# Router logits by token quarter: sixteen accumulating products of 64 columns in place of four of 256 and a summing product

## The chip, the cores and the metric

The kernel runs on one core of one Trainium2 chip. The metric is the time of one execution on the device, in microseconds (us); lower is better. A core has a matrix engine (TensorE: PE for its matmuls and PEld for its weight loads in the profile), a vector engine (DVE), a scalar engine (ACT), GpSimd (POOL), a queue that issues transfers (SyncE, SP), and 16 DMA engines. TensorE reads on-chip memory (SBUF) and writes only accumulators (PSUM, in banks of 512 float32 columns by 128 partitions).

## What is computed

Two stages: a decaying linear attention over 4 batches, 8 heads, 768 positions and head size 64, and a top-1 mixture of 8 experts over its 3072 output rows of 512 features.

```python
for t in range(S):                                   # attention, per batch and head
    state = gamma * state + outer(k[t], v[t])
    y[t] = scale * q[t] @ state
x = y.transpose(0, 2, 1, 3).reshape(3072, 512)

logits = normalized(x) @ normalized(expert_emb).T / tau
expert = argmax(logits, axis=1)                      # one expert for each row
gate = softmax(logits)[expert]
out[rows of e] = gate * (relu(x[rows of e] @ w1[e]) @ w2[e])
```

## The kernel before, in words

The attention stage works in 12 steps `m` (three for each batch, `NCB` = 3) of 256 tokens each. In a step TensorE transposes `k` and `q` of the next step (L365, L383), makes masked scores (L396, masked on DVE at L417), multiplies them with `v` (`intra`, L464), adds what the state contributes (`inter`, L471, recorded at L464 too) and adds to the states (`state`, L431). The result of step `m` is `yTs[m]`, 512 features (4 chunks `j` of 128, on the partitions) by 256 tokens. From there it goes two ways: DVE turns it into rows (`rows_turn`, L493), which SP writes to the buffer `xd` in DRAM (`rows`, L500); and the router works on it.

The router has three parts. `logits_products(m)` (L513) multiplies `enT`, the normalised expert embeddings (128 features by 32 columns of which 8 are experts) with `yTs[m]`. Chunk `j` of the features uses column quarter `j` of the array (32 of 128 columns), so its product of 32 by 256 lands in partitions 32j to 32j+31 of one bank; the four products are partial sums and each is a matmul on its own. `logits_rows(m)` (L521) turns the bank in blocks of 32 by 32 on DVE, so that the tokens come to the partitions: `parts`. `sums(g)` (L531) adds the four partial sums for a group `g` of steps (`GROUPS`: steps 0-2, 3-5, 6-7, 8, 9-10, 11): its left operand `quarters` is a constant of zeros and ones that adds the four partition blocks, and each of its four matmuls writes one quarter of the tokens. `choose` (L545 to L554) then finds maximum and argmax on DVE, `add_counts` (L572 to L576) counts, `count` and `ranks` (L561 to L565 on TensorE, L583 to L588 on DVE, one step later) give each row a slot in its expert's list, and `place` (L597, POOL) writes the row's number to the table `tbl` in DRAM.

All five engines run an order written out by hand; nothing is rearranged. In step `m` TensorE's order is: `count` of the group before, scores, `inter`, `state(m+1)`, `logits_products(m-1)`, transposes of `k`, `q`, `q`, `k` for `m+1`, `sums` if a group ended with step `m-1` (steps 3, 6, 8, 9, 11), then `intra(m)`. In step 3 the products of steps 0, 1 and 2 come together. In step 11 there are no transposes, and `sums` stands between the two halves of `intra`. DVE's order in a step is: `ranks`, masks, `logits_rows`, the sums of states (L444 to L449), `choose`, `add_counts`, `rows_turn(m-1)`.

SP's order matters at the end of the stage. In step 8 it issues the four writes of `rows(7)`, then 12 weight transfers of expert 0 (`load_piece`, L206), then a load of the first slot list (`early_slots`, L635), the writes of `rows(8)`, and two further slot lists. POOL then gathers the first 280 rows of expert 0 from `xd` (`early_gather`, L626, three gathers into `xge`), and SP's next weight transfers (L206, at 109.12 us) are held back until these gathers have landed. TensorE goes on with the transposes of `xge` (L645), the last `logits_products`, and the first layer of expert 0 (L260); from there the seven other experts follow.

Some PSUM room beside the states, `spare(u, j)`, is used as scratch for the router (the names `pst` of `sums`, `choose`, `count`).

Of the kernel before, what the change touches and what calls it, by code (L numbers as in the profile page):

```python
# [11 lines left out]
F32 = mybir.dt.float32  # L12
# [5 lines left out]
ALU = mybir.AluOpType  # L18
AX = mybir.AxisListType
# [5 lines left out]
P = 128  # L25
B, H, S, D = 4, 8, 768, 64
T2 = 2 * P
NCB = S // T2
NM = B * NCB
NB = 2 * NM  # L30
NT = B * S
DM = H * D
NE = 8
DF = 1024
KT = DM // P
FT = DF // P
Q = 32
NQ = P // Q
# [18 lines left out]
NOV = (NT - OV + P - 1) // P  # L57
# [3 lines left out]
def _layout():  # L61
    at, n = {}, 0
    for name, w in (("tq", NCB * 2 * H), ("tk", NCB * 2 * H), ("e16", NE), ("tok", 3),
                    ("ids", 2 * NB), ("quarters", Q), ("ovthr", NOV), ("caps", NE), ("order", NE), ("ranks", NE - 1)):
        at[name] = (n, n + w)
        n += w
    return at, n
# [7 lines left out]
def _constants():  # L75
    c = np.zeros((P, _CW), np.float64)
    p = np.arange(P)
    u, pl = p // 64, p % 64
    g = 1.0 - 2.0 ** (-5.0 - np.arange(H))

    def put(name, a):
        lo, hi = _AT[name]
        c[:, lo:hi] = np.broadcast_to(a, (P, hi - lo))

    t = (T2 * np.arange(NCB)[None, :, None, None] + (P * u + 2 * pl)[:, None, None, None]
         + np.arange(2)[None, None, :, None]).astype(np.float64)

    tt = (T2 * np.arange(NCB)[None, :, None, None] + (8 * (p // KT))[:, None, None, None]
          + np.arange(8)[None, None, None, :]).astype(np.float64)
    gg = g[(2 * (p % KT))[:, None] + np.arange(2)[None, :]][:, None, :, None]  # L90
    put("tq", (gg ** tt / np.sqrt(D)).reshape(P, -1))
    put("tk", (g ** -t).reshape(P, -1))
    put("e16", (np.arange(NE) / 16.0)[None, :])
    put("tok", p[:, None] + P * np.arange(3)[None, :])
    n = np.arange(NB)[None, :]
    put("ids", np.stack([(8 * (p % Q) + p // Q)[:, None] + T2 * (n // 2) + NQ * (n % 2),
                         (4 * (p % Q) + p // Q)[:, None] + P * n], 2).reshape(P, -1))
    put("quarters", (p % Q)[:, None] == np.arange(Q)[None, :])
    put("ovthr", (OV + P * np.arange(NOV))[None, :])
    put("caps", np.array(CAPS)[None, :])  # L100
    put("order", np.arange(NE)[None, :])
    put("ranks", np.array(RANKS)[None, :])
    tri = (p[:, None] < p[None, :]).astype(np.float16)
    return c.astype(np.float32), np.ascontiguousarray(tri)
# [3 lines left out]
def retention_moe(ctx: ExitStack, tc: tile.TileContext, q, k, v, emb, tau, w1, w2, const, const16, out):  # L108
    nc = tc.nc
# [9 lines left out]
    def C(name):  # L119
        lo, hi = _AT[name]  # L120
        return cst1[:, lo:hi] if hi <= _C1 else cst2[:, lo - _C1:hi - _C1]
# [386 lines left out]
    parts = {}  # L508

    def logits_products(m, ps=None):  # L510
        ps = pt_() if ps is None else ps
        for j in range(KT):
            nc.tensor.matmul(ps[j * Q:(j + 1) * Q, :T2], enT[:, j, :], yTs[m][:, j, :], start=True, stop=True,  # L513
                             skip_group_check=True)
        return ps

    def logits_rows(m, ps):
        g = group_of[m]
        if g not in parts:
            parts[g] = ap_.tile([P, max(map(len, GROUPS)), 2, NQ, Q], F32, name="parts")  # L520
        nc.vector.transpose(out=parts[g][:, m - GROUPS[g][0]].rearrange("p u g e -> p (u g) e"),  # L521
                            in_=ps[:, :T2].rearrange("p (g b) -> p g b", b=Q))

    def span(g):
        return slice(2 * GROUPS[g][0], 2 * GROUPS[g][-1] + 2)
# [1 line left out]
    def sums(g, ps=None, fresh=False, room=None):  # L527
        nm = len(GROUPS[g])
        ps = pt_() if ps is None else ps
        for i in range(NQ):  # L530
            nc.tensor.matmul(ps[i * Q:(i + 1) * Q, :2 * nm * NE], C("quarters"),  # L531
                             parts[g][:, :nm, :, i, :NE].rearrange("p m u e -> p (m u) e"), start=not fresh, stop=True,
                             skip_group_check=True)
        at = room if fresh else ps[:, 64:]
        return [a[:, :2 * nm * NE].rearrange("p (n e) -> p n e", e=NE) for a in (ps, at)] + [at[:, 48:48 + NE]]

    chosen = []

    def choose(g, zs):
        z, w, _ = zs  # L540
        r = span(g)
        nb = r.stop - r.start
        bc = lambda t: t.unsqueeze(2).broadcast_to([P, nb, NE])
        m = ap_.tile([P, nb], F32, name="m", bufs=1)
        nc.vector.tensor_reduce(out=m, in_=z, axis=AX.X, op=ALU.max)  # L545
        yield
        nc.vector.tensor_tensor(out=z, in0=z, in1=bc(m), op=ALU.subtract)
        yield
        nc.vector.scalar_tensor_tensor(out=w, in0=z, scalar=0.0,
                                       in1=C("e16").unsqueeze(1).broadcast_to([P, nb, NE]), op0=ALU.is_lt, op1=ALU.add)  # L550
        yield
        nc.vector.tensor_reduce(out=wmn[:, r], in_=w, axis=AX.X, op=ALU.min)
        yield
        chosen.append(nc.vector.tensor_tensor(out=oh[:, r], in0=w, in1=bc(wmn[:, r]), op=ALU.is_equal))  # L554
        yield
# [870 lines left out]
```

## Time and profile before

| | us |
|---|---|
| time, median of 3 runs | 398.85 (398.09 to 399.03) |
| the profiled execution, its own time | 397.74 |
| its span from the first to the last instruction | 395.9 |
| TensorE matmuls busy in the span | 385.1 (97%) |
| VectorE busy | 253.4 (64%) |
| ScalarE busy | 214.6 (54%) |
| GpSimd busy | 153.7 (39%) |

Times in the views count from the start of the span. A timeline row is: start, how long the merged instructions last from the first start to the last end, engine, line, operation, tiles (output <- inputs), shape, count, and in brackets the engine's idle time before it with what ended it. TensorE's matmuls overlap, so the distance from one row's start to the next row's start says what a row costs, not its length. One float32 matmul of the program shows as two records. The line number is that of the helper that records the instruction.

### The profile page before, as it was taken

The page shows a single profiled execution, that of the slowest core. Times are in us where ns is not written, and L with a number is a line of the kernel's source. Part 1 is how long each engine was busy: PE and PEld are TensorE (multiplying, and loading weights), DVE is VectorE, ACT ScalarE, POOL GpSimd, SP SyncE. Part 2 cuts the span into 40 slices and gives each one's busy share as a digit, 9 for nine tenths or more (in the row PEclk, how much of TensorE's full clock was granted, in tenths as well). Part 3 has the DMA queues.
Part 4 walks back from the last instruction along what each step waited for, and adds up shares of the span by engine and source line. Part 5 has one row for each costly group of instructions (what it writes and reads, how often), then busy time and mean ns, then how long its engine had stood idle before and what let it go on. Part 6 is the DMA issues. An engine that isn't in the chain of part 4 may idle for free.

```text
span 395.9 us, 9644 instructions
## 1 busy us (share of the span) xinstructions
PE 385.1 (97%) x3690; PEld 358.9 (91%) x3690; DVE 253.4 (64%) x534; ACT 214.6 (54%) x382; POOL 153.7 (39%) x176
## 2 busy tenths in 40 slices
PE   8999999999999899999999999999999999999993
PEld 4898888988889799999999999999899999999982
DVE  5596876979989358834861963766457656386300
ACT  4585576666847185518544744734855625464420
POOL 2956387688651515204702611520471221211230
PEclk9999999999999999999999999999999999999999
DMA  7998898797468867866868796796998747854121
GB/s 237 271 337 256 238 302 237 217 275 200 121 195 237 282 221 262 280 176 220 265 209 256 251 306 184 236 336 189 273 267 311 206 174 242 234 211 123 39 76 58
DMA packets 91012, 89.20 MB, mean 225 GB/s; under 512 B 10781, under 2 KB 69533, under 8 KB 90956
## 3 DMA queue, kind: packets, MB, share of 16 engines
q1 hardware_dynamic: 85916, 75.39, 63.7%
q0 software_dynamic: 4864, 13.03, 9.1%
q8 instruction: 31, 0.51, 0.5%
q14 instruction: 25, 0.20, 0.2%
q10 hardware_dynamic: 176, 0.07, 0.1%
HBM read 65.00 MB, written 18.79 MB: 212 GB/s over the span
## 4 chain that ended last, share of the span: by engine, by line
PE 82%; issue 7%; DVE 3%; DMA 3%; ACT 1%; POOL 1%; SPq 1%; POOLq 1%
PE b L260 11%; PE pst L1111 11%; PE py L260 9%; PE py L1111 9%; PE py L464 8%; PE pst L260 7%; PE b L396 6%; PE b L1111 4%; PE pst L1153 3%; PE pst L431 3%; PE b L365 3%; PE b L383 2%; DMA raw<-in_moe_w_dram 2%; PE pst L1193 2%; PE b L513 2%
## 5 line engine op out<-in xcount | busy, mean ns | idle before, releaser
L238 DVE TENSOR_TENSOR wlo<-raw,whi 128x1024 fp32r<-128x1024 f32 x64 | 77.7, 1218 | 16.9 <-ACT whi L234 16.5
L1135 POOL DMA_INDIRECT out_dram<-og,si x28 | 29.9, 1068 | 122.5 <-ACT og L1128 71.9
L234 ACT CAST whi<-raw 128x1024 fp32r<-128x1024 f32 x64 | 66.2, 1045 | 4.0 <-DMA raw<-in_moe_w_dram 4.0
L626 POOL DMA_INDIRECT xr<-xd,gi x25 | 30.6, 1223 | 31.7 <-ACT sq L293 15.3
L260 PE MATMUL b<-xh,whi 128*128 128x360 f32 (+5 forms) x104 | 34.3, 334 | 0.0
L260 PE MATMUL b<-xl,whi 128*128 128x360 f32 (+5 forms) x104 | 34.2, 333 | 0.0
L260 PE MATMUL b<-xh,wlo 128*128 128x360 f32 (+5 forms) x104 | 34.1, 332 | 0.0
L417 DVE TENSOR_TENSOR pm<-b,mask 128x512 f32<-128x512 f32 x48 | 29.8, 683 | 4.7 <-PE b L396 4.5
L1094 DVE STREAM_TRANSPOSE xt<-xg 128x384 f32<-128x384 f32 (+1 forms) x28 | 15.6, 578 | 25.5 <-DMA xg<-xs 25.5
L354 POOL TENSOR_TENSOR hh<-whi,cst 128x512 f32<-128x512 f32 x22 | 23.1, 1066 | 20.9 <-DVE pm L417 12.8
L265 ACT ACTIVATE hh<-b 128x360 fp32r<-128x360 f32 (+5 forms) x26 | 12.6, 484 | 33.1 <-PE b L260 33.1
L1111 PE MATMUL pst<-hh,whi 128*128 128x360 f32 (+4 forms) x88 | 29.4, 334 | 0.6 <-ACT hh L265 0.6
L1111 PE MATMUL pst<-hh,wlo 128*128 128x360 f32 (+4 forms) x88 | 29.4, 334 | 0.2 <-DVE wlo L238 0.2
L597 POOL DMA_INDIRECT tbl<-zt,sloti x24 | 25.4, 1056 | 10.8 <-issue 4.2
L1111 PE MATMUL pst<-hl,whi 128*128 128x360 f32 (+4 forms) x88 | 29.4, 334 | 0.1
L260 PE MATMUL py<-xl,whi 128*128 128x384 f32 (+5 forms) x84 | 27.9, 335 | 0.0
L260 PE MATMUL py<-xh,whi 128*128 128x384 f32 (+5 forms) x84 | 27.5, 334 | 0.0
L260 PE MATMUL py<-xh,wlo 128*128 128x384 f32 (+5 forms) x84 | 27.3, 331 | 0.0
L359 POOL TENSOR_TENSOR hl<-wlo,cst 128x512 f32<-128x512 f32 x22 | 22.7, 1047 | 7.8 <-DMA wlo<-in_k_dram 6.8
L396 PE MATMUL b<-qT,kT 64*128 64x128 f32 x384 | 24.7, 278 | 0.0
L464 PE MATMUL py<-pm,vs 128*64 128x128 f32 x384 | 24.1, 276 | 0.0
L1111 PE MATMUL py<-hh,whi 128*128 128x360 f32 (+4 forms) x72 | 23.5, 326 | 0.0
(236 smaller groups left out, 1010.4 us busy)
## 6 DMA issues: line engine op xcount, KB each, us to landing
raw<-in_moe_w_dram SPq DMA_DIRECT2D x60, 512.0 KB
whi<-in_q_dram SPq DMA_DIRECT2D x24, 256.0 KB
xd<-x SPq DMA_DIRECT2D x48, 128.0 KB
wlo<-in_k_dram SPq DMA_DIRECT2D x11, 512.0 KB
xs<-xr SPq DMA_DIRECT2D x6, 768.0 KB
og<-yt SPq DMA_DIRECT2D x72, 48.0 KB
whi<-in_v_dram SPq DMA_DIRECT2D x6, 512.0 KB
wlo<-in_v_dram SPq DMA_DIRECT2D x6, 512.0 KB
```

Of the source, the lines that this page charges most:

```text
L234: nc.scalar.copy(out=views[1], in_=views[0])
L238: nc.vector.tensor_tensor(out=views[2], in0=views[0], in1=views[1].bitcast(F32), op=ALU.subtract)
L260: nc.tensor.matmul(acc[:, :w], a, x[:, kt, cols], start=(n == 0), stop=(n == len(todo) - 1))
L354: return eng.tensor_tensor(out=qs_r[:, m % 3, :, a], in0=qin[m % 3][:, a], in1=w, op=ALU.mult)
L359: return eng.tensor_tensor(out=ks_r[:, m % 3, s, h], in0=kin[m % 3][:, h, s], in1=w[:, h], op=ALU.mult)
L396: nc.tensor.matmul(psc[a][:, j], kTs[m][a * D:(a + 1) * D, j, u].rearrange("p s c -> p (s c)"), q_cols(m, a, j, u), start=True, stop=True, ...
L417: o.append(nc.vector.tensor_tensor(out=pm, in0=psc[a], in1=w, op=ALU.mult))
L464: nc.tensor.matmul(pys[m][u][o * D:(o + 1) * D, j], lhsT, rhs, start=first, stop=True, skip_group_check=True)
L597: i = nc.gpsimd.indirect_dma_start(out=tbl[:, :], out_offset=bass.IndirectOffsetOnAxis(ap=sloti[:, n:n + 1], axis=0), in_=zt[:, n], in_off ...
L626: return nc.gpsimd.indirect_dma_start(out=xr[:n, j, :], out_offset=None, in_=xd[:rows_, :], in_offset=bass.IndirectOffsetOnAxis(ap=gi[:n, ...
L1111: nc.tensor.matmul(acc[:, :c], a[:, f], x[:, kt, :c], start=(n == 0), stop=(n == 3 * FT - 1))
L1135: i = nc.gpsimd.indirect_dma_start(out=out[:, :], out_offset=bass.IndirectOffsetOnAxis(ap=si[:n, e, j:j + 1], axis=0), in_=og[:n, j, :], i ...
```

## The change

`logits_products` now also splits the tokens: each of the four feature chunks `j` makes four matmuls, one for each quarter `i` of the tokens (64 columns: two blocks of 32, one of each half of the step), and quarter `i` of the array's columns always takes quarter `i` of the tokens. The four chunks add up in the accumulator (`start` at the first, `stop` at the last). So 16 matmuls of 64 columns stand where 4 of 256 stood, the bank holds 64 finished columns in place of 256 columns of partial sums, `logits_rows` turns 64 columns in place of 256, and `parts` is a quarter as large. `sums` makes no matmuls any more (4 in each of 6 groups are left out) and only hands out the scratch room. `choose` reads `parts` in SBUF where it read the sums in PSUM, and its row maxima `m` lie in PSUM scratch in place of SBUF. The constant `quarters` is left out.

```diff
     def logits_products(m, ps=None):
         ps = pt_() if ps is None else ps
         for j in range(KT):
-            nc.tensor.matmul(ps[j * Q:(j + 1) * Q, :T2], enT[:, j, :], yTs[m][:, j, :], start=True, stop=True,
-                             skip_group_check=True)
+            y = yTs[m][:, j].rearrange("p (u g b) -> p g u b", u=2, b=Q)
+            for i in range(NQ):
+                nc.tensor.matmul(ps[i * Q:(i + 1) * Q, :2 * Q].rearrange("p (u b) -> p u b", b=Q), enT[:, j, :], y[:, i],
+                                 start=(j == 0), stop=(j == KT - 1), skip_group_check=True)
         return ps
...
-            parts[g] = ap_.tile([P, max(map(len, GROUPS)), 2, NQ, Q], F32, name="parts")
-        nc.vector.transpose(out=parts[g][:, m - GROUPS[g][0]].rearrange("p u g e -> p (u g) e"),
-                            in_=ps[:, :T2].rearrange("p (g b) -> p g b", b=Q))
+            parts[g] = ap_.tile([P, max(map(len, GROUPS)), 2, Q], F32, name="parts")
+        nc.vector.transpose(out=parts[g][:, m - GROUPS[g][0]], in_=ps[:, :2 * Q].rearrange("p (u b) -> p u b", b=Q))
...
     def sums(g, ps=None, fresh=False, room=None):
         nm = len(GROUPS[g])
         ps = pt_() if ps is None else ps
-        for i in range(NQ):
-            nc.tensor.matmul(ps[i * Q:(i + 1) * Q, :2 * nm * NE], C("quarters"),
-                             parts[g][:, :nm, :, i, :NE].rearrange("p m u e -> p (m u) e"), start=not fresh, stop=True,
-                             skip_group_check=True)
         at = room if fresh else ps[:, 64:]
-        return [a[:, :2 * nm * NE].rearrange("p (n e) -> p n e", e=NE) for a in (ps, at)] + [at[:, 48:48 + NE]]
+        return [a[:, :2 * nm * NE].rearrange("p (n e) -> p n e", e=NE) for a in (ps, at)] + [at[:, 48:48 + NE], at[:, 56:56 + 2 * nm]]
...
     def choose(g, zs):
-        z, w, _ = zs
+        z, w, _, m = zs
...
-        m = ap_.tile([P, nb], F32, name="m", bufs=1)
-        nc.vector.tensor_reduce(out=m, in_=z, axis=AX.X, op=ALU.max)
-        yield
-        nc.vector.tensor_tensor(out=z, in0=z, in1=bc(m), op=ALU.subtract)
+        s = parts[g][:, :nb // 2, :, :NE].rearrange("p m u e -> p (m u) e")
+        nc.vector.tensor_reduce(out=m, in_=s, axis=AX.X, op=ALU.max)
+        yield
+        nc.vector.tensor_tensor(out=z, in0=s, in1=bc(m), op=ALU.subtract)
```

Nothing else moves: ACT, POOL and SP have the same instructions in the same order. Two places show it. The first is TensorE in step 8, from the products of step 7 to `intra` (`b` are banks, `hl` and `hh` the scaled `k` and `q`, `pst` the scratch). Before:

```order
L513 MATMUL b_1617<-yT,enT 32x256 x4
L365 MATMUL b_1627<-ident,hl 128x128 x4
L383 MATMUL b_1635<-ident,hh 128x128 x4
L383 MATMUL b_1641<-ident,hh 128x128 x4
L365 MATMUL b_1648<-ident,hl 128x128 x4
L531 MATMUL pst_1567<-parts,cst_61 32x32 x4
L464 MATMUL py_1519<-pm_1531,vs 64x128
```

and in the changed kernel (its line numbers are one to four off):

```order
L514 MATMUL b_1691<-yT,enT 32x64 x16
L364 MATMUL b_1713<-ident,hl 128x128 x4
L382 MATMUL b_1721<-ident,hh 128x128 x4
L382 MATMUL b_1727<-ident,hh 128x128 x4
L364 MATMUL b_1734<-ident,hl 128x128 x4
L463 MATMUL py_1593<-pm_1605,vs 64x128
```

The four summing matmuls between the last transposes and `intra` are gone, and the product has 16 short matmuls. The second place is DVE in the same step, from `logits_rows(7)` into `choose`. Before:

```order
L521 STREAM_TRANSPOSE parts<-b_1617 128x256
L446 COPY s_1623<-pst_1567 128x256
L449 TENSOR_TENSOR s_1625<-pst_1567,tB 128x256
L545 TENSOR_REDUCE m<-pst_1567 128x4
L547 TENSOR_TENSOR pst_1567<-pst_1567,m 128x32
L549 SCALAR_TENSOR_TENSOR pst_1567<-pst_1567,cst_61 128x32
```

and in the changed kernel:

```order
L522 STREAM_TRANSPOSE parts<-b_1691 128x64
L445 COPY s_1709<-pst_1641 128x256
L448 TENSOR_TENSOR s_1711<-pst_1641,tB 128x256
L541 TENSOR_REDUCE pst_1641<-parts 128x4
L543 TENSOR_TENSOR pst_1641<-parts,pst_1641 128x32
L545 SCALAR_TENSOR_TENSOR pst_1641<-pst_1641,cst_61 128x32
```

The order is the same, but the first instruction of `choose` reads what DVE itself wrote two instructions earlier, where it read what TensorE wrote.

## Rows read from the trace of the kernel before

**Rows 1.** Engines by stretch: stretch, length, busy us of each engine, clock, DMA.
```profile
36.00:111.00 75.00, 74.75 (x1500) 65.23 (x1498) 62.25 (x153) 49.12 (x87) 52.07 (x55) 1.00 0.80 226
111.00:138.00 27.00, 25.21 (x201) 23.14 (x198) 19.42 (x55) 11.15 (x24) 12.91 (x15) 1.00 0.81 245
138.00:357.00 219.00, 218.97 (x1231) 213.87 (x1230) 138.70 (x258) 120.44 (x215) 61.48 (x61) 1.00 0.77 242
```

**Rows 2.** Timeline of PE in step 7, which has no sums.
```profile
74.99 0.60 PE L365 MATMUL b<-ident,hl 128*128 128x128 f32 x4
75.52 0.66 PE L464 MATMUL py<-pm,vs 128*64 128x128 f32 x8
```

**Rows 3.** Timeline of PE in step 3.
```profile
40.77 0.60 PE L365 MATMUL b<-ident,hl 128*128 128x128 f32 x4
...
41.53 0.33 PE L464 MATMUL py<-pm,vs 128*64 128x128 f32 x2
```

**Rows 4.** Timeline of PE in step 8.
```profile
83.30 0.60 PE L365 MATMUL b<-ident,hl 128*128 128x128 f32 x4
83.83 0.27 PE L531 MATMUL pst<-parts,cst 128*32 128x32 f32 x8
84.03 1.97 PE L464 MATMUL py<-pm,vs 128*64 128x128 f32 x32
```

**Rows 5.** Timeline of PE in step 9.
```profile
92.15 0.60 PE L365 MATMUL b<-ident,hl 128*128 128x128 f32 x4
92.99 0.25 PE L531 MATMUL pst<-parts,cst 128*32 128x16 f32 x8 [0.25 <-DVE s L449]
93.18 1.97 PE L464 MATMUL py<-pm,vs 128*64 128x128 f32 x32
```

**Rows 6.** Timeline of PE in step 11.
```profile
107.15 1.09 PE L464 MATMUL py<-pm,vs 128*64 128x128 f32 x16
108.17 0.27 PE L531 MATMUL b<-parts,cst 128*32 128x32 f32 x8
...
109.40 0.44 PE L645 MATMUL pst<-ident,xge 128*128 128x128 f32 x2
```

**Rows 7.** Chain of waits, steps 3 to 5: start, time on the chain, what.
```profile
38.04 1.43 PE b L513 x24
...
47.70 0.57 PE b L513 x8
...
50.16 1.90 PE py L464 x32
...
55.08 0.93 PE pst L431 x64
```

**Rows 8.** Timelines of PE and of PEld, both cut at 64.2 to 64.3.
```profile
64.24 0.42 PE L513 MATMUL b<-yT,enT 128*32 128x256 f32 x4
...
64.24 0.16 PEld L513 LDWEIGHTS b<-yT,enT 128*32 128x32 f32 x8
```

**Rows 9.** Timeline of DVE in step 8.
```profile
84.17 0.19 DVE L545 TENSOR_REDUCE m<-pst 128x4 f32<-128x32 f32 x1 [1.01 <-PE pst L531]
...
85.74 1.30 DVE L493 STREAM_TRANSPOSE x<-yT 128x512 f32<-128x512 f32 x2
```

**Rows 10.** Timeline of SP's queue, steps 8 to 11.
```profile
87.08 2.58 SPq L500 DMA_DIRECT2D xd<-x  x4
89.70 7.44 SPq L206 DMA_DIRECT2D raw<-in_moe_w_dram  x12
...
97.70 3.44 SPq L500 DMA_DIRECT2D xd<-x  x4
```

**Rows 11.** Timeline of POOL, steps 10 and 11.
```profile
99.54 1.01 POOL L597 DMA_INDIRECT tbl<-zt,sloti  x1 [0.90 <-PE pst L431]
...
102.75 1.58 POOL L626 DMA_INDIRECT xge<-xd,gi  x1 [0.49 <-DMA xd<-x]
```

**Rows 12.** Waits of SP's queue: who waited for whom, total, times, longest.
```profile
SPq L206 <- DMA xge<-xd,gi: 5.3, 1, 5.3
```

**Rows 13.** Chain of waits behind the attention stage.
```profile
118.50 6.00 DMA raw<-in_moe_w_dram
```

More of the change, by code (lines that the diff above doesn't have):

```diff
@@ L63, in _layout @@
     for name, w in (("tq", NCB * 2 * H), ("tk", NCB * 2 * H), ("e16", NE), ("tok", 3),
-                    ("ids", 2 * NB), ("quarters", Q), ("ovthr", NOV), ("caps", NE), ("order", NE), ("ranks", NE - 1)):
+                    ("ids", 2 * NB), ("ovthr", NOV), ("caps", NE), ("order", NE), ("ranks", NE - 1)):
         at[name] = (n, n + w)
@@ L97, in _constants @@
                          (4 * (p % Q) + p // Q)[:, None] + P * n], 2).reshape(P, -1))
-    put("quarters", (p % Q)[:, None] == np.arange(Q)[None, :])
     put("ovthr", (OV + P * np.arange(NOV))[None, :])
```

## Prediction

> **What bounds the kernel now.** I read the busy times by stretch first. In the attention stage TensorE is busy for 74.75 of 75 us, in the seven later experts for 218.97 of 219, and only in the 27 us between does it stand idle, for 1.8 us [rows 1]. So what TensorE is spared in the attention stage moves everything behind it, provided that the stretch of 27 us follows too. That stretch is not TensorE's: the chain of waits goes there through SP's transfers, with 6.00 us for a piece of expert 0's weights [rows 13]. SP's weight transfers stand still for 5.3 us until the gathers of expert 0's first rows have landed, at about 109.1 us [rows 12], and TensorE takes up these rows at 109.40 [rows 6]. Two clocks therefore have to move: TensorE's arrival at 109.40 and the landing of the gathers. Third I read the timeline of TensorE in a step with and in one without `sums`, and fourth what DVE, SP and POOL wait for on the way to the gathers. [...]
>
> **The summing products are left out.** From the last transposes to `intra` TensorE takes 0.53 us in step 7, which has no sums [rows 2]. With sums it is 0.76 us in step 3 [rows 3], 0.73 in step 8 [rows 4] and 1.03 in step 9 [rows 5]. The extra is 0.23, 0.20 and 0.50 us; step 6 repeats step 3 (48 columns again), 0.23. Little of it is streaming: by the rounds worked out below (0.054 us for 64 columns) the two rounds of 32 columns in step 8 are 0.05 us of the 0.20; the rest is the way into the quarter columns and out of them again. In step 9 0.25 us are a wait: `sums` writes scratch beside the states and waits for DVE's sum of states [rows 5]. `intra`, next in line, does not need that, so the wait goes with the product. What is late next there is the transposes, which TensorE does anyway. In step 11 the sums cut `intra` in two: 2.25 us from its start to the next work [rows 6], 1.90 uncut [rows 7], so 0.35. The sixth group stands in the first layer of expert 0, inside the stretch that SP's transfers bound; I count it at nothing (its cover is the weight stream; without that cover it would bring about what step 8 brings, 0.20). **Sum: 0.23 + 0.23 + 0.20 + 0.50 + 0.35 = 1.51 us before 109.40.**
>
> **The products of 64 columns.** Six rounds of four concurrent products cost 1.43 us on the chain and two cost 0.57 [rows 7]: (1.43 - 0.57) / 4 = 0.215 us for a round of four times 256 columns, and 0.57 - 0.43 = 0.14 us that comes once (first load, change of tiling, drain). The new product has 16 x 2 = 32 records, 8 rounds of four times 64 columns. In proportion a round is 0.215 / 4 = 0.054 us. The nearest row with 64 columns in concurrent tiles is `state`: 64 records in rounds of four, 0.93 / 16 = 0.058 us [rows 7]. So a product costs 0.14 + 8 x (0.054 to 0.058) = 0.57 to 0.60 us where it cost 0.57. I take 0.59, 0.02 more each, nearer to `state` since that has the same column count. There are eleven products before 109.40 (the twelfth lies in the covered stretch): **0.22 us given back, with ends 0 and 0.33.** It must not be forgotten that the columns stay the same (4 x 256 = 16 x 64): what is added is records, 32 for 8, and weight loads, 32 for 8.
>
> What could make a round longer is the weights: each of the 32 records loads its own. In the trace all eight loads of a product had begun before 64.3 and were done 0.16 us after 64.24, when only the first four matmuls had started, and these run on until 64.66 [rows 8]: the second round's loads go in beside the first round's matmuls. With 64 columns a round is shorter, but so is the time that loads may take: eight in 0.16 us is 0.08 us for four if they went one behind another, over the 0.054 of a round. As they overlap each other in that row, I take them as hidden, and keep the 0.08 for a rival. [...]
>
> **VectorE.** `logits_rows` turns a quarter of the columns, which can only help; I count it at nothing, since TensorE is not waiting for it. `choose` reads SBUF in place of PSUM in two of five instructions, and writes its maxima the other way round; 0.19 us for the reduction now [rows 9], some 0.02 either way, and nobody on TensorE waits for it. What counts is that it no longer waits: in step 8 DVE stands idle for 1.01 us until `sums` is done [rows 9], and everything behind it on DVE, `rows_turn(7)` above all, follows that much earlier.
>
> **SP, POOL and the gathers.** `rows_turn(7)` ends at 87.04, and SP's writes start at 87.08 [rows 9, 10]. SP then issues for ten microseconds with hardly a break, 12 weight transfers and the writes of `rows(8)` [rows 10]; the first gather waits 0.49 us for the last of those writes [rows 11]. So this chain can start 1.0 us earlier by DVE's wait alone, and another 0.46 by steps 3 and 6 less nine products (9 x 0.02 = 0.18): about 1.3. POOL's own chain is released by `state` in step 10 [rows 11], after the gains of steps 3, 6, 8 and 9: 0.23 + 0.23 + 0.20 + 0.50 - 10 x 0.02 = 0.96, and has the 0.49 to spare: up to 1.45. The gathers land 1.0 to 1.4 us earlier. TensorE is at 109.40 by 1.51 - 0.22 = 1.29 us earlier and finds its rows there, or nearly so.
>
> **The sum.** 1.3 us, with the transfers behind following: the span 395.9 - 1.3 = 394.6, the profiled execution 397.74 - 1.3 = 396.4. That execution was 1.1 us under the median of the runs, which is what will be compared: 398.85 - 1.3 = 397.5. About 0.3% (1.2 us) is what a measurement here can tell from no change, so the forecast stands at the edge of being seen.
>
> **Rivals.** (a) *TensorE is spared the time but the transfers don't follow.* SP's ten microseconds from 89.70 are a queue that takes 7.44 us for 12 transfers [rows 10]; if the DMA engines set its pace (0.80 of them busy over the stage [rows 1]), starting it earlier only makes it wait longer. Then the gathers follow only what steps 3 and 6 release, 0.46 less 0.18 for the products, 0.3 us: 398.5. For it: the DMA share. Against it: the gathers' last condition is a landing of a few transfers, and 0.49 us is POOL's to spare. (b) *Weights come into the open*, the one that ends slower: each of the 88 rounds before 109.40 waits for its four loads. The gain is gone when a round lasts 1.51 / 88 = 0.017 us over 0.054, and it is slower by 1.2 us from 0.031 on. With 0.08 us for loads that do not overlap the matmuls at all the price is 7.0 us and the time 404.4; half of it gives 3.5 - 1.5, 400.9. Against it: the overlap in [rows 8]. (c) *The sixteen don't run four abreast*, so the change doesn't do what it says: 32 x 0.054 + 0.14 = 1.87 us a product, 1.3 more, times eleven 14 us: 412. Against it: `state` interleaves in just this order, four tiles inside and the accumulation outside, and keeps 0.058 a round [rows 7]. (d) *More than the sum*: the wait of DVE in step 8 also holds the masks of step 9, and every transfer behind the gathers has less to collide with; with the sixth group's 0.2 and 0.5 to 1 us in the 27 us stretch, where TensorE idles 1.8 us, 396.5.
>
> **Chances.** The forecast (396.9 to 398.2) has 0.50, (a) 0.30, (d) 0.10, (b) 0.08, (c) 0.02. The range takes in the forecast, (a) and most of (d): 396.6 to 399.1; it leaves out (b), (c) and the far end of (d). Faster by over 0.3% means under 397.65: a little more than 0.6 of the forecast's half, nearly all of (d) and a little of (a), which such a run-to-run spread allows: 0.46. Slower by over 0.3% is (b) and (c), less what a mild (b) would leave within: 0.08. Within: 0.46.
>
> **What the new profile would show.** Right: `intra` starts 0.53 us after the last transposes begin in steps 3, 6, 8 and 9; two products follow each other at the distance of now, 0.57 to 0.60 on the chain; `choose` follows DVE's sum of states with no wait; TensorE starts the transposes of `xge` near 108.1 and SP the weights behind the gathers near 107.9. (a) shows TensorE idle before the transposes of `xge`, or the same idle time as now plus a full microsecond behind 124 us. (b) shows the distance from one round of products to the next at 0.07 us or more, with loads starting only as matmuls end. The prediction is wrong if the products take over 0.70 us each, or if SP's writes of `rows(7)` still start around 87.

## The result: slower, by 0.64%

The changed kernel takes 401.38 us (median of 10 runs, 400.15 to 405.24), the kernel before 399.12 beside it (10 runs, 396.9 to 400.21): ratio 1.0064, interval 1.0038 to 1.009. The prediction was 397.5 with a range up to 399.1. The profiled execution of the changed kernel took 401.72 us with a span of 400.0; that of before 397.74 and 395.9.

In the changed kernel's lines the logits products stand at L514 (L513 before), the transposes of k at L364 (L365), `intra` and `inter` at L463 (L464), the transposes of the gathered rows at L641 (L645), SP's weight transfers at L205 (L206). Engines by stretch, as in [rows 1] (stretch, length, busy us of PE, PEld, DVE, ACT, POOL, clock, DMA share, GB/s):

```profile
36.00:111.00 75.00, 71.95 (x1701) 66.35 (x1701) 58.89 (x145) 47.38 (x84) 51.91 (x52) 1.00 0.82 228
111.00:138.00 27.00, 24.61 (x220) 22.52 (x217) 20.64 (x62) 12.96 (x26) 11.19 (x15) 1.00 0.83 239
138.00:357.00 219.00, 218.22 (x1229) 212.51 (x1228) 135.19 (x254) 119.43 (x214) 63.14 (x65) 1.00 0.79 241
```

TensorE, which stood idle for 0.25 us of the attention stage, now does so for 3.05. The waits of TensorE name one place for it (line, what it waited for: us in total, times, longest):

```profile
PE b L514 <- issue: 3.1, 2, 2.8
...
PE b L259 <- DVE wlo L237: 0.7, 1, 0.7
PE pst L641 <- DMA xge<-xd,gi: 0.4, 1, 0.4
```

"issue" is a wait that the profile shows no releaser for. The timeline of step 3, where three products follow one another, shows where it lies (start, us, engine and line, count, idle time before it):

```profile
37.92 0.86 PE L514 MATMUL b<-yT,enT 128*32 128x64 f32 x43
38.64 0.25 DVE L522 STREAM_TRANSPOSE parts<-b 128x64 f32<-128x64 f32 x1 [0.96 <-PE b L514]
...
41.62 0.98 PE L514 MATMUL b<-yT,enT 128*32 128x64 f32 x53 [2.84 <-issue]
41.63 0.81 PEld L514 LDWEIGHTS b<-yT,enT 128*32 128x32 f32 x52 [3.00 <-issue]
42.20 0.25 DVE L522 STREAM_TRANSPOSE parts<-b 128x64 f32<-128x64 f32 x1 [3.31 <-PE b L514]
```

43 of the 96 matmuls run, then matmuls and weight loads both stand still for 2.84 us in the middle of the second product, and DVE has to wait for its end. No operand is late: the last yT of the three was copied by 34.9, and enT is older still. Step 8 has a second, shorter stop (0.21 us, after 23 of 32 matmuls). The rest of the attention stage went as forecast. The timeline of TensorE from the last transposes of k to `intra` in steps 7, 8 and 9, and of `intra` of step 11 up to the gathered rows:

```profile
77.73 0.60 PE L364 MATMUL b<-ident,hl 128*128 128x128 f32 x4
78.26 1.97 PE L463 MATMUL py<-pm,vs 128*64 128x128 f32 x32
...
86.48 0.60 PE L364 MATMUL b<-ident,hl 128*128 128x128 f32 x4
87.01 1.97 PE L463 MATMUL py<-pm,vs 128*64 128x128 f32 x32
...
95.03 0.60 PE L364 MATMUL b<-ident,hl 128*128 128x128 f32 x4
95.56 1.97 PE L463 MATMUL py<-pm,vs 128*64 128x128 f32 x32
...
109.56 1.97 PE L463 MATMUL py<-pm,vs 128*64 128x128 f32 x32
111.45 0.76 PE L641 MATMUL pst<-ident,xge 128*128 128x128 f32 x2
112.60 0.66 PE L641 MATMUL pst<-ident,xge 128*128 128x128 f32 x4 [0.38 <-DMA xge<-xd,gi]
```

The distances are 0.53 us in all three steps, where step 8 had 0.73 [rows 4] and step 9 1.03 [rows 5]; step 11 takes 1.89 us where it took 2.25 [rows 6].

**Where the time went.** TensorE reaches the gathered rows at 111.45 instead of 109.40, 2.05 us later. The two stops took 3.06 and 0.43 us from record to record, 3.49 together; so its own work is 1.44 us shorter. But the gathered rows follow the stops and not the gain. SP and POOL on the way to them, from the timeline of all engines (answers to [rows 10 to 12]):

```profile
89.07 2.60 SPq L499 DMA_DIRECT2D xd<-x  x4
...
91.71 8.27 SPq L205 DMA_DIRECT2D raw<-in_moe_w_dram  x12
...
103.18 3.71 SPq L631 DMA_DIRECT2D tb<-tbl  x2
...
105.00 1.78 POOL L622 DMA_INDIRECT xge<-xd,gi  x1 [0.28 <-POOL gi L616]
...
112.57 1.28 SPq L205 DMA_DIRECT2D raw<-in_moe_w_dram  x3
```

The writes of `rows(7)` start 1.99 us later than in [rows 10] and the first gather 2.25 later than in [rows 11], so both are over a microsecond ahead of the stops. Then it is lost again: the 12 weight transfers take 8.27 us instead of 7.44, and SP goes on behind the gathers at 112.57, 3.45 us later than the 109.12 of before: all of the stops, nothing of the gain. TensorE waits for the rows (0.38 us and a shorter gap before it) and, from 140 to 200 us, stands 2.9 us behind the kernel before. Another 1.0 us is lost in expert 3, with a wait of 0.7 us for `wlo` in the list above, and the end is 4.1 us later. Between the medians it is 2.3 us; the profiled execution of before was 1.4 us faster than its median.

### The profile page after: what moved, and what is told of

It is laid out like the page before. It is cut to its first block, busy times and chain, and to the rows that moved or that the text cites. A ratio compares the mean times of both kernels' runs of the same rounds, so it can differ in the third digit from the quotient of the medians.

```text
span 400.0 us, 10124 instructions
## 1 busy us (share of the span) xinstructions
PE 385.2 (96%) x3930; PEld 362.2 (91%) x3930; DVE 252.1 (63%) x534; ACT 214.7 (54%) x382; POOL 153.7 (38%) x176
## 4 chain that ended last, share of the span: by engine, by line
PE 69%; DMA 8%; issue 7%; SPq 5%; DVE 5%; ACT 2%; POOL 2%; POOLq 0%; ACTq 0%; DVEq 0%
PE b L259 9%; PE pst L1107 8%; PE py L1107 8%; PE py L259 7%; PE py L463 7%; PE pst L259 6%; PE b L395 4%; SPq L1119 4%; DMA raw<-in_moe_w_dram 4%; PE b L1107 3%; PE pst L1149 3%; PE pst L430 2%; PE b L382 2%; PE b L364 2%; PE pst L1189 1%
## 5 line engine op out<-in xcount | busy, mean ns | idle before, releaser
L1131 POOL DMA_INDIRECT out_dram<-og,si x28 | 29.0, 1036 | 128.4 <-DMA xg<-xs 59.4
L1091 ACT CAST xh<-xt 128x384 fp32r<-128x384 f32 (+4 forms) x28 | 14.3, 511 | 20.1 <-DVE xt L1090 19.8
L463 PE MATMUL py<-pm,vs 128*64 128x128 f32 x384 | 23.9, 276 | 0.0
```

Source lines behind the costliest of these rows:

```text
L463: nc.tensor.matmul(pys[m][u][o * D:(o + 1) * D, j], lhsT, rhs, start=first, stop=True, skip_group_check=True)
L1131: i = nc.gpsimd.indirect_dma_start(out=out[:, :], out_offset=bass.IndirectOffsetOnAxis(ap=si[:n, e, j:j + 1], axis=0), in_=og[:n, j, :], i ...
```

## Experiments

All times are medians, with the kernel before run beside them. "Stop" is idle time of TensorE in its profile.

**Where do the stops come from?** Theory 1: TensorE runs out of instructions. The profile counts the packets of a queue that it calls "instruction" (packets, MB, share), 33 of them now and 31 before, of 16,384 bytes each (before, then changed):

```profile
q8 instruction: 31, 0.51, 0.5%
q8 instruction: 33, 0.54, 0.6%
```

That is one transfer for some 240 records of TensorE (weight loads and matmuls, 7,380 before and 7,860 now). A product was 8 loads and 8 matmuls, and is now 32 and 32. Theory 2 puts the loss on the transfers behind or, later, on the chip.

The first four kernels were to tell the number of instructions from the new layout. `e1` cuts only the three products of step 3 (the other steps as before), `e2` only those of the later steps:

```
-        for j in range(KT):
-            nc.tensor.matmul(ps[j * Q:(j + 1) * Q, :T2], enT[:, j, :], yTs[m][:, j, :], ...)
+        n = NQ if m < 3 else 1        # e2: m >= 3
+        for i in range(n):
+            c = slice(i * T2 // n, (i + 1) * T2 // n)
+            for j in range(KT):
+                nc.tensor.matmul(ps[j * Q:(j + 1) * Q, c], enT[:, j, :], yTs[m][:, j, c], ...)
```

> The kernel before, with one change: the three router products that step 3 makes back to back (those of steps 0 to 2) are each cut along the tokens into 16 matmuls of 64 columns in place of 4 of 256, with the same layout, the same sums and the same results. Theory 1 (TensorE runs out of instructions: the changed kernel's trace shows 2.84 us of idle time in the middle of these three products, put down to nothing that the trace shows as a releaser): the same idle time of 2 to 3 us appears in step 3, and the time is 2 to 3 us over the kernel before. Theory 2 (the loss comes from the transfers behind the attention stage, and the idle time in step 3 belongs to that one execution): no idle time, at most 0.2 us slower.

Measured 402.12 us beside 401.16, ratio 1.004 (1.0013 to 1.0067). The stop is there, in step 3, with the old layout and the sums in place, though shorter than the 2 to 3 us that theory 1 said:

```profile
PE b L516 <- issue: 0.8, 1, 0.8
```

> The kernel before, with the router products of steps 3 to 11 cut into 16 matmuls of 64 columns each, those of steps 0 to 2 as before. Theory 1: the cut itself costs 9 x 0.015 us, since these products stand alone between longer matmuls; within 0.5 us of the kernel before, with at most one short idle time (0.2 us, as the changed kernel shows in step 8). Theory 2: slower by 2 us or so, as every product moves the transfers behind.

Measured 408.93, ratio 1.0207 (1.0178 to 1.0236). Both theories missed: no stop in step 3, but three others of about 2 us each, in steps 9 and 10 and in expert 0, where TensorE waits for DVE's `parts`. They are taken up below.

`e3` is the changed kernel with the first group (step 3's products and its sums) as before, `e4` the kernel before with only that group changed; both by a condition on `group_of[m]` in `logits_products`, `logits_rows`, `sums` and `choose`.

> The changed kernel, with the first group (steps 0 to 2, whose products stand back to back in step 3) in the old form: 4 matmuls of 256 columns each and the summing product. Theory 1: the idle time of 2.84 us in step 3 is gone, what is left of the forecast is 1.51 - 0.23 - 8 x 0.015 = 1.16 us, so 1 us faster than the kernel before, and some 3 us faster than the changed one. Theory 2: about as slow as the changed kernel, 2 us over the kernel before.

> The kernel before, with the first group alone (steps 0 to 2) in the new form: 16 matmuls of 64 columns for each of the three products of step 3, no summing product for that group. Theory 1: TensorE idle for 2 to 3 us in step 3, 0.23 us spared by the summing product, so 2 to 2.8 us slower than the kernel before. Theory 2: within 0.3 us of the kernel before.

`e4`: 401.47, ratio 1.0017 (0.9994 to 1.0039): a stop of 1.3 us in step 3, and a time that can't be told from that of the kernel before, where theory 1 said 2 to 2.8 us more. `e3`: 407.27, ratio 1.0147 (1.0115 to 1.0178). It was to be 1 us faster than the kernel before and is 6 us slower. Its step 3 has no stop, as theory 1 wants, but steps 9 and 10 and expert 0 have those of `e2`, and step 5 has one that was not expected (timeline of PE):

```profile
56.78 0.65 PE L520 MATMUL b<-yT,enT 128*32 128x64 f32 x32
57.37 0.44 PE L365 MATMUL b<-ident,hl 128*128 128x128 f32 x2
59.65 0.44 PE L365 MATMUL b<-ident,hl 128*128 128x128 f32 x2 [1.84 <-issue]
```

It stands inside four equal transposes of ready operands. Counting TensorE's records from the start of each trace, those of its semaphore instructions included, settled what these places share. The stops come at record 1473 in the changed kernel, in `e1` and in `e4`, at 3521 in the changed kernel's step 8, and at 2241 in `e3`. All of these are 193 plus a multiple of 256. By these traces, then, TensorE's instructions come in pieces of 256 (64 bytes each, by 16,384 / 256), and the transfer of a piece mostly starts when the piece before it has been begun (median 1.2 us behind its begin, in the 235 pieces counted below). For the pieces that end at a stop, and the same piece of the kernel before (us; worked out from the traces):

```
kernel            records      piece     transfer starts  takes   usable after   stop
                               lasted    after its begin          its end
before            1217-1473    5.72      1.69             0.95    (not waited)   0
changed           1217-1473    3.02      3.65             0.88    1.54           3.06
e1                1217-1473    3.02      1.58             0.95    1.46           0.97
e4                1217-1473    3.02      2.33             0.95    1.23           1.49
changed, step 8   3265-3521    2.93      1.06             0.88    1.42           0.43
e3, step 5        1985-2241    2.70      2.40             0.94    1.47           2.11
```

In these five stops a piece was used up before 1.23 to 1.54 us had passed after the end of its successor's transfer, and the stop is what was left of that time. Stop or not, in none of the 235 pieces that begin up to 112 us in the 14 traces does a record run sooner than 1.23 us after the end of its transfer. With the shortest delay here this needs 1.06 + 0.88 + 1.42, 3.4 us, with the longest 6.1. A piece with three new products in it lasts 3.0.

**Moving the borders.** If this is right, the same work must stop elsewhere, or not at all, when some instructions are put ahead of everything. `e7` and `e8` do that in the warm-up; `e5` and `e6` are the two kernels as they are.

```
-    for _ in range(W0):                       # 10 of 512 columns
-        nc.tensor.matmul(idle, zeros[:, :P], zeros, start=True, stop=True)
+    for _ in range(42):                       # e8: 98 of 52 columns
+        nc.tensor.matmul(idle[:, :122], zeros[:, :P], zeros[:, :122], start=True, stop=True)
```

> The kernel before, unchanged, with a profile of its own beside the three others, so that what this chip does to either kernel is not taken for an effect of an edit. Theory 1 (TensorE's instructions come in pieces of 256, and TensorE stops where a piece is used up before the next has come): no piece of this kernel lasts under 5 us up to layer 2, so there is no stop of TensorE by issue over 0.3 us in steps 3 to 11, ratio 1.000 +- 0.003. Theory 2 (the stops belong to the chip, or to the traffic of the hour): stops of 1 to 3 us here too.

> The changed kernel, unchanged. Theory 1: the piece that begins at TensorE's record 1217 lasts 3.0 us (its transfer needs 0.9 us, 1.6 to 3.7 us pass before it starts and 1.2 to 1.5 us after it has ended), so TensorE stops at record 1473 in step 3 again, for 0.7 to 3.1 us; ratio to the kernel before 1.003 to 1.009. Theory 2: the stop is elsewhere or gone.

> The changed kernel with 42 idle products of 122 columns at its start in place of 10 of 512 (5,124 columns for 5,120): 64 more records of TensorE (32 weight loads, 32 products) ahead of everything, so that every border between two pieces of 256 falls 64 records earlier in the work. Nothing else is changed. By the times of the records of the changed kernel the shortest piece in steps 3 to 11 would then last 4.4 us instead of 2.9. Theory 1: no stop over 0.5 us in step 3 and none in step 8, 2 to 3.5 us less than the changed kernel, ratio to the kernel before 0.997 to 1.000. Theory 2 (the stop comes from the three products behind one another, or from the busy DMA queues, wherever the borders are): the stop stays, the time is that of the changed kernel within 0.5 us.

> The same with 98 idle products of 52 columns (5,096 columns): 176 more records, so that the borders fall 176 records earlier, the first of step 3's dense pieces begins at record 1297 of the old count and lasts 2.0 us instead of 3.0. Theory 1: the stop of step 3 moves from the second product to the transposes behind the products, about 80 records later in the work, and is about 1 us longer (1.9 to 4 us), with a second one of 0.5 to 2 us in step 5 (a piece of 3.4 us); step 8's is gone; ratio to the kernel before 1.006 to 1.013. Theory 2: as the changed kernel, within 0.5 us.

Measured beside 400.32 us: `e5` 401.32 (1.001, 0.9984 to 1.0036), `e6` 406.73 (1.0156, 1.0124 to 1.0189), `e7` 404.77 (1.0128, 1.0084 to 1.0171), `e8` 407.49 (1.0196, 1.0153 to 1.0239). Where the stops of this kind lie is as theory 1 says: at borders alone. The times are not: `e6`, `e7` and `e8` are all above the ranges that it gave them. `e6` stops at record 1473 for 2.47 us (transfer begun after 3.08) and at 3521 for 0.71. `e7` has no stop at any border; its step 3 runs through, all 96 matmuls in one piece of time:

```profile
39.12 1.55 PE L514 MATMUL b<-yT,enT 128*32 128x64 f32 x96
```

In `e8` the stop of step 3 has moved to the third product (it was to lie behind the products), that of step 5 is 0.1 us where 0.5 to 2 were expected, and a stop of 1.1 us that was not expected has appeared in the state matmuls of step 2, where the changed kernel had none:

```profile
40.47 1.42 PE L514 MATMUL b<-yT,enT 128*32 128x64 f32 x83
43.32 0.42 PE L514 MATMUL b<-yT,enT 128*32 128x64 f32 x13 [1.44 <-issue]
```

By the medians the 64 records ahead are worth 2.0 us and the 176 cost 0.8, but the intervals of all three overlap. And `e6` and `e7` keep a loss that the borders don't explain and that the changed kernel's first trace does not have: in this later comparison the changed kernel loses 1.6%, not 0.6%.

**The clock behind a stop.** One part of that loss is TensorE's clock. Engines by stretch behind the stop of step 3, columns as in the first table, `e6` and then the changed kernel's first trace:

```profile
41.00:44.30 3.30, 3.13 (x60) 2.95 (x60) 1.55 (x6) 0.28 (x1) 0.00 (x0) 0.50 0.91 273
41.60:45.00 3.40, 3.38 (x79) 3.12 (x80) 2.39 (x10) 1.72 (x4) 0.00 (x0) 1.00 0.95 302
```

In `e6` TensorE stood idle for 2.25 us up to 41.17; the granted clock is at 0.50 from 41.0 to 44.4 and then at 1.00 again. In the first trace it stays at 1.00, though the idle time was 2.84 us. The 256 records from 1473 on take 7.55 us in `e6` and 6.07 in the first trace, so this stop cost 1.5 us more than its own length. `e2`, `e3`, `e4`, `e7`, `e8`, `f0`, `f1` and `f2` have one or two such stretches at 0.50 as well, at or within 2 us behind a wait of TensorE; the kernel before, `e5`, `e1` and `f3` have none between 36 and 140 us. Why the clock is lower behind one stop and not behind another is open.

**The second stop.** In step 9 of `e6` (timeline of all engines; "remote" is a release that the profile cannot name):

```profile
94.10 1.88 DVE L416 TENSOR_TENSOR pm<-b,mask 128x512 f32<-128x512 f32 x3
...
94.99 0.65 PE L514 MATMUL b<-yT,enT 128*32 128x64 f32 x32
...
96.08 1.04 PE L382 MATMUL b<-ident,hh 128*128 128x128 f32 x8
...
98.93 0.25 DVE L522 STREAM_TRANSPOSE parts<-b 128x64 f32<-128x64 f32 x1 [2.95 <-remote]
...
99.24 0.66 PE L364 MATMUL b<-ident,hl 128*128 128x128 f32 x4 [2.12 <-issue]
```

The product's last matmul is over at 95.64, and TensorE goes on with transposes until 97.12. DVE, free since 95.98, begins to turn the product only at 98.93. Of TensorE's semaphore the trace has an update at 95.10 and the next at 98.91, 3.3 us after the product; in the kernel before it came 0.04 us after it (90.72, 90.76). Five matmuls with an update end between 95.64 and 97.12, and five updates come from 98.91 to 99.78, so these records are late and not missing. So here TensorE has its instructions; its signal is late, and TensorE, whose next transposes wait for DVE's semaphore, then stands still behind it. `e2`, `e3`, `e6`, `e7` and `e8` have this stop in steps 9 and 10 and in expert 0, 1.4 to 2.8 us each. `e5` has not, in the same places on the same chip (the same view of step 9):

```profile
90.44 0.64 PE L513 MATMUL b<-yT,enT 128*32 128x256 f32 x8
...
91.53 1.16 PE L383 MATMUL b<-ident,hh 128*128 128x128 f32 x8
91.89 0.44 DVE L521 STREAM_TRANSPOSE parts<-b 128x256 f32<-128x256 f32 x1
...
92.52 0.60 PE L365 MATMUL b<-ident,hl 128*128 128x128 f32 x4
```

The last four kernels ask what causes it. `f0` is `e7` once more. `f1` is the kernel before with idle matmuls ahead of each product from step 4 on, so that only the number of instructions is that of cut products:

```
+        for i in range(3 if m >= 3 else 0):
+            for j in range(KT):
+                nc.tensor.matmul(ps[j * Q:(j + 1) * Q, T2:T2 + 64], enT[:, j, :], yTs[m][:, j, :64], ...)
         for j in range(KT):
             nc.tensor.matmul(ps[j * Q:(j + 1) * Q, :T2], enT[:, j, :], yTs[m][:, j, :], ...)
```

`f2` is `e7` with the product moved behind the transposes of q, and `f3` is `e7` with the new form for the first two groups alone:

```
-            for i in () if m < 3 else (0, 1, 2) if m == 3 else (m - 1,):
-                logits_rows(i, logits_products(i))
+            if m == 3:
+                for j in range(3):
+                    logits_rows(j, logits_products(j))
...
+                if m > 3:
+                    logits_rows(m - 1, logits_products(m - 1))
                 transpose_k(m + 1, 1)
...
             else:
+                logits_rows(m - 1, logits_products(m - 1))
                 intra(m, 0)
```

> The changed kernel with 64 more TensorE records at its start (42 idle products of 122 columns for 10 of 512) once more, as the measure for the two variants of it beside it. Theory 1 (the stops of step 3 and 8 come from the borders between pieces of 256 instructions): again no stop there. Theory 3 (TensorE's signal comes late after a product of 16 matmuls in steps 9, 10 and in expert 0, where GpSimd's indirect DMAs start at the same time): three stops of 1.4 to 2.8 us on a chip whose trace lacks a tenth of the semaphore updates, ratio to the kernel before 1.008 to 1.015; on a chip whose trace lacks none, 0.996 to 1.000.

> The kernel before with 12 idle matmuls of 64 columns (into columns that nothing reads) ahead of the four of 256 columns of each product from step 4 on, and ahead of steps 3's none: the products, their layout and the sums stay as they were, only the number of TensorE's instructions is that of the products cut in four. The idle ones cost 3 rounds of 0.056 us for each of 9 products, 1.5 us if all lie on the path. Theory 3a (the late signal comes from the number of instructions in the burst): stops of 1.4 to 2.8 us in steps 9, 10 and expert 0 as in the changed kernel, ratio 1.012 to 1.022. Theory 3b (it comes from the products' own form, four column groups that write to one another's columns in turn): no such stop, ratio 1.000 to 1.005.

> The changed kernel with 64 more records at its start, and from step 4 on each product issued behind the transposes of q (1.5 us later in its step) instead of right behind the 32 state matmuls: the same instructions, no longer two dense bursts behind one another and no longer at the start of GpSimd's first indirect DMA. Theory 3a: the stops of steps 9 and 10 are gone or under 0.7 us, expert 0's stays; 2.5 to 4 us less than the run beside it that differs in this alone. Theory 3b, or a signal late for whatever product is in those steps: the stops move with the product, the time within 1 us of that run.

> The changed kernel's products and left-out sums for the first two groups of tokens alone (products of steps 3 to 6), the kernel before's for the other four, and 64 more records at the start. Theory 1 with theory 3: neither the stop of steps 3 and 8 (borders moved) nor those of steps 9, 10 and expert 0 (old products there) remain, and two groups' sums (0.23 us each) are spared: ratio 0.997 to 1.001. If the new products cost something of their own in steps 3 to 6 (a lengthening beside the stops): 1.002 to 1.006.

Measured beside 400.76 us: `f0` 405.44 (1.0144, 1.0107 to 1.0181); `f1` 409.72 (1.0223, 1.0185 to 1.0261); `f2` 404.6 (1.0104, 1.0063 to 1.0144); `f3` 402.03 (1.0031, 1.0006 to 1.0057).

`f1` decides for the number of instructions and against the form of the new products. Its products are the old ones, of 256 columns, and the stops are there, 1.2 to 2.0 us each. Its time also has up to 1.5 us of idle matmuls in it and a stop of 0.8 us at a border in step 5. The same view of step 9 (L514 are the idle ones, L517 the product):

```profile
93.91 0.54 PE L514 MATMUL b<-yT,enT 128*32 128x64 f32 x24
94.27 0.61 PE L517 MATMUL b<-yT,enT 128*32 128x256 f32 x8
...
95.32 1.04 PE L383 MATMUL b<-ident,hh 128*128 128x128 f32 x8
...
97.82 0.45 DVE L525 STREAM_TRANSPOSE parts<-b 128x256 f32<-128x256 f32 x1 [3.04 <-PE b L383]
...
98.32 0.66 PE L365 MATMUL b<-ident,hl 128*128 128x128 f32 x4 [1.97 <-issue]
```

`f2` takes TensorE's stops of steps 9 and 10 away with the same instructions in another place; expert 0's stays, 1.6 us. Step 9 (timeline of all engines):

```profile
94.53 0.97 POOL L593 DMA_INDIRECT tbl<-zt,sloti  x1 [0.30 <-issue]
94.85 0.65 PE L514 MATMUL b<-yT,enT 128*32 128x64 f32 x32
95.44 0.66 PE L364 MATMUL b<-ident,hl 128*128 128x128 f32 x4
...
97.66 0.25 DVE L522 STREAM_TRANSPOSE parts<-b 128x64 f32<-128x64 f32 x1 [2.26 <-remote]
```

Over steps 9 and 10 it gains 3.3 us on `f0`. It gives 1.2 of them back in steps 5 and 6, why was not followed up, and its wait for expert 1's rows is 1.7 us where `f0` has 0.8; the whole is 0.8 us faster, not the 2.5 to 4 that theory 3a expected. And the signal of step 9 is still late: the product is over at 95.50, and DVE, free since 95.40, turns it at 97.66. TensorE has other work in the meantime and stops there for under 0.3 us at a time. So the move shows what a late signal costs, and not that the place behind the states makes it late.

What makes it late can be narrowed down from the traces. Call a signal late by the time from the product's end, or from the end of DVE's work before if that is later, to DVE's `logits_rows` (worked out from the traces). In `e2`, `e3`, `e6`, `e7`, `e8`, `f0` and `f1` a GpSimd indirect DMA runs during the products of steps 7 to 10 and of expert 0. All 35 of these signals are late, by 0.6 to 3.3 us, those of steps 7 and 8 too, where TensorE does not stop for them. None runs during the products of steps 4, 5, 6 and 11, and those 28 signals are late by 0.07 us at most, although the products of steps 4 to 6 stand right behind the states just the same. In step 6 `f2` has put a product away from the states and beside an indirect DMA, and its signal, 0.07 us late in `f0`, is 1.98 us late:

```profile
67.13 0.65 PE L514 MATMUL b<-yT,enT 128*32 128x64 f32 x32
...
67.67 1.01 POOL L593 DMA_INDIRECT tbl<-zt,sloti  x1 [0.15 <-issue]
...
69.76 0.25 DVE L522 STREAM_TRANSPOSE parts<-b 128x64 f32<-128x64 f32 x1 [3.10 <-PE py L463]
```

So of the two neighbours, the states ahead and the indirect DMAs beside it, it is the indirect DMAs that go with the late signal. No run took them away, so this is a coincidence in 36 products and no proof of the cause. A product of 8 loads and 8 matmuls in the same places is late by 0.7 us at most (`e1`, `e4`, `e5`, `f3`), and the changed kernel's first trace by 0.5.

What holds the signal isn't shown either. The traces of the three later comparisons hold 6,976 to 7,200 semaphore updates, those of the first pair 7,952 and 7,959, for nearly the same program. All signals that are more than 0.7 us late are in traces that lack records in this way, but `e1`, `e4`, `e5` and `f3` lack as many (6,996 to 7,047) and have no such signal. A common cause is possible; no run here tells whether the recording plays a part, and every time of this study was taken with it.

`f3` has no signal over 0.5 us late, but theory 1's claim for it failed: a stop of 1.34 us in step 4, at a border (record 1985), in a piece of 4.9 us:

```profile
47.81 0.52 PE L520 MATMUL b<-yT,enT 128*32 128x64 f32 x19
49.67 0.42 PE L520 MATMUL b<-yT,enT 128*32 128x64 f32 x13 [1.34 <-issue]
```

The transfer started 3.96 us into the piece; in `f0` it was 0.61 at the same border and there was no stop. When the transfer starts varies from run to run, from 1.0 us ahead of the piece's begin to 4.5 us behind it (median 1.2 behind, over the 235 pieces). In all of them there are 12 stops of 0.3 us or more from record to record at a border, in pieces of 2.0 to 4.9 us; the kernel before's shortest piece from step 3 to step 11 lasts 4.9 us, and it has none in its two traces.

## Why the prediction was wrong

**The step that failed is the price of the products of 64 columns.** It said "what is added is records, 32 for 8, and weight loads, 32 for 8", and then asked only whether the loads stay hidden. Records have a price of their own here: TensorE is supplied with 256 at a time, and at two borders it stood still for 3.06 and 0.43 us. The term of 0.22 us (0 to 0.33) was 0.17 plus 3.49 us of stops. No rival held this, though the profile of before showed the instruction queue; rival (b) at half its price comes to 400.9 and so near the measured 401.38 by chance, as its mechanism is out (below). A bound would have been in reach: 192 records in 1.5 us in step 3, against 256 in 4.9 us or more in every piece of before from there to step 11.

- **The clock:** the forecast has no term for it. In the changed kernel's first trace none was needed: the clock stayed at 1.00 through 2.84 us of idle time. In `e6` it was at 0.50 behind 2.25 us, and 256 records took 1.5 us longer.
- **The summing products:** right. Steps 3, 6, 8, 9 and 11 gave 0.23, 0.23, 0.20, 0.50 and 0.36 us against 1.51 in sum; the wait in step 9 went with its product, as forecast.
- **The products themselves:** right while they are supplied. From a product's start to the next operation are 0.585 us, where it was 0.57; a round is 0.056 us. Rivals (b) and (c) are out. The loads stay beside the matmuls: in step 4 the 32 loads of a product take 0.49 us and its 32 matmuls 0.65, both from 50.53 on. And the four run abreast, as one after another they would have taken 1.87 us by the prediction's estimate.
- **TensorE's arrival:** right, 1.44 us of work less where 1.29 was forecast, hidden under the stops.
- **VectorE:** right. The wait of 1.01 us in step 8 [rows 9] is gone.
- **The gathers:** wrong. They were to land 1.0 to 1.4 us earlier. Measured against the stops, SP's and POOL's chain began that much earlier and landed no earlier. This is rival (a): 12 weight transfers took 0.8 us more and the two reads of `tb` 3.71 us instead of 2.46.
- **Rival (a)** had a chance of 0.30. In this trace the gain would have been mostly lost behind 109 us even without the stops; one trace does not say how often.
- **One count:** eight products, not nine, lie ahead of step 8's `rows_turn`; that is 0.02 us and changes nothing.

The loss behind 200 us (the 1.0 us in expert 3) was not looked into; the wait for `wlo` is also in `e6` and not in `e5`. No version here beats the kernel before: as recorded here, the instructions that the change adds cost more than the sums that it saves.

## To carry to other kernels

Count records as well as columns: cutting the matmuls into smaller ones that run abreast cost 0.015 us a product on the array here, and 3.49 us of stops in supply in the changed kernel's first trace. Wherever an edit makes TensorE denser, list the stretch that every 256 records last, and hold it against what the transfers of the instruction queue take from the border to their use (3.4 to 6.5 us at the stops here); instructions put far ahead move all borders (64 records in `e7`, and step 3 had no stop). An edit that saves 1.5 us by adding 480 records should be tried with dummy records first.

## What the runs showed of the hardware

- In the 14 traces TensorE's instructions arrived in transfers of 16,384 bytes, 256 records. In the 235 pieces up to 112 us a transfer took 0.88 to 1.78 us (median 0.97) and started from 1.0 us ahead of the piece before it to 4.5 us after that piece had been begun, and no piece was used sooner than 1.23 us after its transfer's end. Where the piece before was used up earlier, matmuls and weight loads both stopped, in the changed kernel in the middle of a product (12 stops, 0.3 to 3.1 us from record to record).
- Behind one stop the clock was lower: in `e6` the granted clock is 0.50 from 41.0 to 44.4 us, behind 2.25 us of idle time, and 256 records took 7.55 us there against 6.07 at 1.00. Behind another it was not: 2.84 us in the changed kernel's first trace left it at 1.00.
- In step 9 of `e6` TensorE's semaphore update came 3.3 us after the end of its product, while TensorE went on working until 97.12; three late updates then came 0.06 us apart (99.66, 99.72 and 99.78). Signals 0.6 to 3.3 us late came with groups of 32 loads and 32 matmuls that had a GpSimd indirect DMA beside them, in the three later comparisons; in the first the lateness was 0.5 us at most.
- The same edit cost 0.6% in one comparison and 1.6% in another, with the kernel before at 399.12 and 400.32 us.
